# Expert tiles of 128 slots with three weight buffers, in place of 256 slots with two

## The chip, the cores and the metric

One core of a Trainium2 chip runs the whole kernel in one launch. Its engines are TensorE (PE; its weight loads are shown apart as PEld), VectorE (DVE), ScalarE (ACT), GpSimd (POOL) and SyncE (SP), and DMA queues that SyncE and GpSimd feed. The metric is the device time of one execution in microseconds (us), taken as the median of several runs. Everything is computed in float32.

## The reference

```python
scores = scale * q @ k.T ; masked by 32 x 32 blocks           # B=4, H=8, S=768, D=64
x = softmax(scores) @ v                                       # to (3072, 512)

xn = x / (norm(x) + 1e-6); en = expert_emb / (norm(expert_emb) + 1e-6)
logits = xn @ en.T / tau                                      # 8 experts
expert_idx = argmax(logits); gate_w = softmax(logits)[expert_idx]
for e in range(8):
    h = maximum(x[mask_e] @ w1[e], 0.0)                       # 512 -> 1024
    out[mask_e] = gate_w[mask_e] * (h @ w2[e])                # 1024 -> 512
```

Attention with a block mask gives 3072 rows of 512 values. Each row is sent to one of eight experts, a pair of matrices with a ReLU between them, and the result is multiplied by the row's gate.

## The kernel before

The program has three stages. **Attention** runs over 192 units (4 sequences, 8 heads, 6 chunks of 128 queries): `score` multiplies a chunk by the keys (L184), `turn_probs` transposes the exponentials on TensorE (L201), `attend` multiplies them by the values (L219). After each sequence `route` finds every row's expert, gate and rank and writes the rows with their gates to `x_dram`. **`dispatch`** then sorts: it gives every row a slot in expert order, each expert's rows being padded to a multiple of `G` slots. `NG` is the largest number of tiles that any routing can need, (3072 + 8 * (G - 1)) // G, and the loop over tiles always runs to `NG`: 19 tiles at G = 256. Tiles that hold no row are computed like the others.

**The expert stage** is the one that the change touches. `fetch(i)` issues what tile i needs: SyncE issues two DMAs of 2 MB, `w1` (L354) and `w2` (L356), from the expert whose number it has read into a register, and GpSimd issues one indirect DMA for each 128 slots (L361), which gathers rows from `x_dram`. `expert_tile(i)` then

- transposes the gathered rows on TensorE into `xg_ps` (L375) and copies them to `xgt`, one half by VectorE (L378) and one by ScalarE (L379);
- multiplies them by `w1` into `hp` (L386): 8 blocks `f` of 128 hidden values, each a sum over 4 pieces `d`, in two PSUM tiles of four blocks. `w1` is the stationary operand, and the slots are the moving columns, 256 of them. When four blocks are done, ScalarE takes the ReLU of two of them (L388) and VectorE of the other two (L389), into `h`;
- multiplies `h` by `w2` into `yp` (L394), 128 slots at a time: `h` is stationary, 512 columns of `w2` move, summed over the 8 blocks `f`;
- multiplies by the gate on VectorE into `y` (L397) and has GpSimd scatter `y` to the output by an indirect DMA (L399).

Every float32 matmul of the program but the transposes stands in the trace as two records, each with a weight load of its own, so the 32 matmuls of L386 are 64 records a tile and the 16 of L394 are 32; a transpose is one record. Weights lie in a pool of two buffers each for `w1` and `w2`, and `fetch(i + 1)` stands ahead of `expert_tile(i)` in the program. Each engine works through its own instructions in program order; semaphores, put in by the tile framework, order the engines among each other.

Of the kernel before, what the change touches and what calls it, by code (L numbers as in the profile page):

```python
# [10 lines left out]
F32 = mybir.dt.float32  # L11
I32 = mybir.dt.int32
ACT = mybir.ActivationFunctionType
ALU = mybir.AluOpType
# [3 lines left out]
P = 128  # L18
B, H, S, D = 4, 8, 768, 64
BLK = 32  # L20
NB = S // BLK  # attention blocks per sequence
NRAND = 3
NC = S // P  # chunks of 128 tokens; token p * NC + c of a sequence is row p of chunk c
NPAIR = H // 2
N = B * S
NT = B * NC
DM, E, F = H * D, 8, 1024
ND, NF = DM // P, F // P
G = 256  # slots of an expert tile: every expert's tokens are padded to a multiple of it
GS = G // P  # L30
NG = (N + E * (G - 1)) // G  # the most expert tiles that any routing can need
NS = NG * GS
XW = DM + 1  # a token's row: its activations and its gate
SCALE = 1.0 / float(D) ** 0.5
NEG = -1.0e9

# [40 lines left out]


def build_mask(k):
    """Rows that extend the contraction of q and k: the key's block one-hot against the  # L80
    query block's mask row (0 where it attends, NEG where not)."""
    nc, pool = k.nc, k.setup
    ids = pool.tile([NB, NRAND], I32, name="ids")
    words = dataclasses.replace(k.blocks.tensor, shape=[NB, 2 * NRAND], dtype=I32)
    with nc.allow_non_contiguous_dma(reason="low words of the block numbers"):
        nc.sync.dma_start(out=ids, in_=bass.AP(tensor=words, offset=0, ap=[[2 * NRAND, NB], [2, NRAND]]))
    ids_f = pool.tile([NB, NRAND], F32, name="ids_f")
    nc.vector.tensor_copy(out=ids_f, in_=ids)

    dif = iota(k, "dif", [NB, NB], [[1, NB]], mult=-1)  # L90
    col = iota(k, "col", [NB, NB], [[1, NB]])
    row = iota(k, "row", [NB, NB], [[0, NB]], mult=1)
    m = pool.tile([NB, NB], F32, name="m")
    nc.vector.tensor_tensor(out=m, in0=dif, in1=dif, op=ALU.mult)
    nc.vector.tensor_scalar(out=m, in0=m, scalar1=1.5, scalar2=None, op0=ALU.is_le)
    for val in (0.0, float(NB - 1)):
        for pos in (col, row):
            nc.vector.scalar_tensor_tensor(out=m, in0=pos, scalar=val, in1=m, op0=ALU.is_equal, op1=ALU.max)
    for r in range(NRAND):
        nc.vector.scalar_tensor_tensor(out=m, in0=col, scalar=ids_f[:, r:r + 1], in1=m,  # L100
                                       op0=ALU.is_equal, op1=ALU.max)
    nc.vector.tensor_scalar(out=m, in0=m, scalar1=1.0, scalar2=-NEG, op0=ALU.subtract, op1=ALU.mult)

    oh = pool.tile([P, NC, NB], F32, name="oh_blk")
    nc.gpsimd.memset(oh, 1.0)
    nc.gpsimd.affine_select(out=oh, in_=oh, pattern=[[1, NC], [-BLK, NB]], compare_op=ALU.is_ge,
                            fill=0.0, base=0, channel_multiplier=NC)
    nc.gpsimd.affine_select(out=oh, in_=oh, pattern=[[-1, NC], [BLK, NB]], compare_op=ALU.is_ge,
                            fill=0.0, base=BLK - 1, channel_multiplier=-NC)
    kr = k.big.tile([P, 1024], F32, name="kr", tag="big")  # L110
    for c in range(NC):
        nc.tensor.transpose(kr[0:NB, c * P:(c + 1) * P], oh[:, c, :], k.ident)
    krow = pool.tile([NB, S], F32, name="krow")
    nc.vector.tensor_copy(out=krow, in_=kr[0:NB, 0:S])
    qr = k.big.tile([P, 1024], F32, name="qr", tag="big")
    for lo, hi in ((0, 512), (512, S)):
        nc.tensor.matmul(qr[0:NB, lo:hi], lhsT=m, rhs=krow[:, lo:hi], start=True, stop=True)

    k.sides = []
    for i in range(2):  # L120
        side = {}
        for name, rows, copy in (("q", qr[0:NB, 0:S], nc.scalar.copy), ("k", krow, nc.vector.tensor_copy)):
            for h in range(2):
                side[name, h] = k.const.tile([D + NB, S], F32, name=f"{name}{h}_{i}")
                copy(out=side[name, h][D:D + NB, :], in_=rows)
        k.sides.append(side)
# [103 lines left out]


def route(k, b):
    """Expert, gate and rank within the expert for the tokens of one sequence."""
    nc, p, x = k.nc, k.rp, k.x[b]
    nrm = p.tile([P, NC], F32, name="nrm")
    for c in range(NC):
# [7 lines left out]
    for c2 in range(0, NC, 2):  # L244
        ps = k.big.tile([P, 2 * ND, P], F32, name="xt_ps", tag="big")
        for i in range(2 * ND):
            c, d = c2 + i // ND, i % ND
            nc.tensor.transpose(ps[:, i, :], x[:, c, d * P:(d + 1) * P], k.ident)
        xt = p.tile([P, 2 * ND, P], F32, name="xt")
        nc.vector.tensor_copy(out=xt, in_=ps)  # L250
        for c in (c2, c2 + 1):
            for d in range(ND):
                nc.tensor.matmul(lg[:, c, :], lhsT=xt[:, (c - c2) * ND + d, :], rhs=k.en[:, d, :],
                                 start=(d == 0), stop=(d == ND - 1))

    def wide(t):
# [15 lines left out]
    gate = p.tile([P, NC], F32, name="gate")  # L272
# [5 lines left out]
        out=k.x_dram[b * S:(b + 1) * S, :].rearrange("(p c) w -> p (c w)", c=NC),  # L278
        in_=x.rearrange("p c w -> p (c w)"),
    )  # L280

    for c in range(NC):
        t = b * NC + c
# [6 lines left out]


def dispatch(k):
    """Slots in expert order: the token of each slot (N where none is), the expert of each tile."""
    nc, p = k.nc, k.dp
    cp = k.small.tile([P, 512], F32, name="cp", tag="small")
    nc.tensor.matmul(cp[:, 0:E], lhsT=k.ones, rhs=k.seen[:, NT, :], start=True, stop=True)
# [6 lines left out]
    need = p.tile([P, E], F32, name="need")  # L303
# [46 lines left out]
def fetch(k, i):  # L350
    nc = k.nc
    e = nc.values_load(k.expert[0:1, i:i + 1], engines=(mybir.EngineType.SP,), min_val=0, max_val=E - 1)
    w1 = k.wp.tile([P, ND, F], F32, name="w1", tag="w1")
    nc.sync.dma_start(out=w1, in_=k.w1[bass.ds(e, 1), :, :].rearrange("o (c p) f -> p (o c) f", p=P))  # L354
    w2 = k.wp.tile([P, NF, DM], F32, name="w2", tag="w2")
    nc.sync.dma_start(out=w2, in_=k.w2[bass.ds(e, 1), :, :].rearrange("o (c p) m -> p (o c) m", p=P))  # L356
    xs = []
    for s in range(GS):
        x = k.gp.tile([P, XW], F32, name="xg", tag="xg")
        t = i * GS + s  # L360
        nc.gpsimd.indirect_dma_start(  # L361
            out=x[:, :], out_offset=None, in_=k.x_dram[:, :],
            in_offset=bass.IndirectOffsetOnAxis(ap=k.slot[:, t:t + 1], axis=0),
        )
        xs.append(x)
    k.fetched[i] = (w1, w2, xs)


def expert_tile(k, i):
    nc = k.nc  # L370
    w1, w2, xs = k.fetched.pop(i)
    ps = k.big.tile([P, ND, GS, P], F32, name="xg_ps", tag="big")
    for d in range(ND):
        for s in range(GS):
            nc.tensor.transpose(ps[:, d, s, :], xs[s][:, d * P:(d + 1) * P], k.ident)  # L375
    xt = k.mp.tile([P, ND, G], F32, name="xgt", tag="xgt")
    half = ND // 2
    nc.vector.tensor_copy(out=xt[:, 0:half], in_=ps[:, 0:half].rearrange("p d s t -> p d (s t)"))  # L378
    nc.scalar.copy(out=xt[:, half:ND], in_=ps[:, half:ND].rearrange("p d s t -> p d (s t)"))  # L379

    h = k.mp.tile([P, NF, G], F32, name="h", tag="h")
    for f0 in range(0, NF, 4):
        hp = k.big.tile([P, 4, G], F32, name="hp", tag="big")
        for f in range(4):
            for d in range(ND):
                nc.tensor.matmul(hp[:, f, :], lhsT=w1[:, d, (f0 + f) * P:(f0 + f + 1) * P], rhs=xt[:, d, :],  # L386
                                 start=(d == 0), stop=(d == ND - 1))
        nc.scalar.activation(h[:, f0:f0 + 2], hp[:, 0:2], ACT.Relu)  # L388
        nc.vector.tensor_scalar(out=h[:, f0 + 2:f0 + 4], in0=hp[:, 2:4], scalar1=0.0, scalar2=None, op0=ALU.max)  # L389

    for s in range(GS):
        yp = k.small.tile([P, DM], F32, name="yp", tag="small")
        for f in range(NF):
            nc.tensor.matmul(yp, lhsT=h[:, f, s * P:(s + 1) * P], rhs=w2[:, f, :],  # L394
                             start=(f == 0), stop=(f == NF - 1))
        y = k.gp.tile([P, DM], F32, name="y", tag="y")
        nc.vector.tensor_scalar(out=y, in0=yp, scalar1=xs[s][:, DM:XW], scalar2=None, op0=ALU.mult)  # L397
        t = i * GS + s
        nc.gpsimd.indirect_dma_start(  # L399
            out=k.out[:, :], out_offset=bass.IndirectOffsetOnAxis(ap=k.slot[:, t:t + 1], axis=0),  # L400
            in_=y[:, :], in_offset=None, bounds_check=N - 1, oob_is_err=False,
        )


@with_exitstack
def kernel(
# [14 lines left out]
    n = Net()  # L421
# [38 lines left out]

    with tc.tile_pool(name="dp", bufs=1) as n.dp:
        dispatch(n)
    n.wp = ctx.enter_context(tc.tile_pool(name="wp", bufs=2))
    n.gp = ctx.enter_context(tc.tile_pool(name="gp", bufs=4))
    n.mp = ctx.enter_context(tc.tile_pool(name="mp", bufs=2))
    fetch(n, 0)
    for i in range(NG):
        if i + 1 < NG:
            fetch(n, i + 1)
        expert_tile(n, i)  # L470


# [30 lines left out]
```

## Time and profile before

| what | us |
|---|---|
| median of 3 runs (lowest, highest) | 1352.59 (1351.52, 1358.27) |
| profiled execution, its span | 1351.6 |
| PE busy in the span | 1293.4 |
| PEld busy | 989.1 |
| DVE, ACT, POOL busy | 410.5, 358.3, 89.4 |

The profiled execution is shown by its span, from the first to the last instruction. The times of the runs are counted for a whole execution, and their median stands 1.0 us above the span. A row of the timeline gives start, duration, engine, line, operation, tiles and how many instructions were merged; in brackets stands how long the engine was idle before it, and which instruction ended that. The durations of matmul records overlap, so the pace of TensorE is read from the starts of the groups that follow each other, and not from the durations.

### The profile page before, as it was taken

Reading aid. Unit: us, or ns where it says so; the run is one execution under the profiler, and the core shown is the slowest. Engines: PE = TensorE matmul, PEld = TensorE weight load, DVE = VectorE, ACT = ScalarE, POOL = GpSimd, SP = SyncE. Lnnn points to the kernel's source line nnn. Section 1 sums busy time; section 2 is a strip of 40 time slices with the busy share of each in tenths; the row PEclk is TensorE's granted clock in tenths of the full one; section 3 lists DMA queues with packets and bytes.
Section 4 is the critical chain, followed back from the end, with each engine's and each line's share of the span. In section 5 each row is a group of like instructions: output and inputs, shape, how many; then the busy total and the mean of one; then the engine's idle time right before and its main releaser. Section 6 shows DMA issues by size and latency. Waiting matters only on the chain. (4 is left out here: it accounts for less than half of the span.)

```text
span 1351.6 us, 16579 instructions
## 1 busy us (share of the span) xinstructions
PE 1293.4 (96%) x6952; PEld 989.1 (73%) x6952; DVE 410.5 (30%) x619; ACT 358.3 (27%) x660; POOL 89.4 (7%) x125
## 2 busy tenths in 40 slices
PE   6999999999999999999999499999999999999997
PEld 4888888888888888888888466666666666666664
DVE  4444453444444444444444401111111111111110
ACT  3444443444434444444444000000000000000000
POOL 1000000000000000000000101111111111111110
PEclk9999998999979999899999589999999999999999
DMA  3010111111011010110000375544544554454420
GB/s 129 24 36 13 36 36 51 33 36 36 24 60 36 24 36 13 36 48 12 1 1 1 122 283 170 201 161 152 192 170 171 177 202 165 145 197 170 148 71 0
DMA packets 49696, 122.24 MB, mean 90 GB/s; under 512 B 3660, under 2 KB 15948, under 8 KB 49110
## 3 DMA queue, kind: packets, MB, share of 16 engines
q1 hardware_dynamic: 43542, 104.89, 22.1%
q0 software_dynamic: 6080, 16.28, 3.4%
q8 instruction: 55, 0.90, 0.3%
q14 instruction: 19, 0.16, 0.0%
HBM read 108.56 MB, written 16.27 MB: 92 GB/s over the span
## 5 line engine op out<-in xcount | busy, mean ns | idle before, releaser
L184 PE MATMUL sc<-k,q 88*128 88x512 f32 (+1 forms) x768 | 294.6, 506 | 0.0
L386 PE MATMUL hp<-xgt,w 128*128 128x256 f32 x1216 | 270.4, 383 | 14.9 <-DVE xgt L378 14.9
L219 PE MATMUL av<-vld,et 128*128 128x64 f32 x2304 | 278.8, 271 | 0.3 <-ACT et L206 0.3
L189 DVE TENSOR_REDUCE nm<-sc 128x1 f32<-128x768 f32 x192 | 183.9, 958 | 296.9 <-PE sc L184 296.6
L219 PEld LDWEIGHTS av<-vld,et 128*128 128x128 f32 x2304 | 272.3, 192 | 0.5 <-ACT et L206 0.5
L386 PEld LDWEIGHTS hp<-xgt,w 128*128 128x128 f32 x1216 | 231.5, 192 | 50.8 <-DVE xgt L378 19.6
L394 PE MATMUL yp<-w,h 128*128 128x512 f32 x608 | 264.0, 592 | 0.0
L191 ACT ACTIVATE e<-sc,nm 128x768 f32<-128x768 f32 x192 | 173.5, 904 | 172.0 <-DVE nm L189 172.0
L394 PEld LDWEIGHTS yp<-w,h 128*128 128x128 f32 x608 | 115.5, 190 | 137.3 <-issue 136.3
L184 PEld LDWEIGHTS sc<-k,q 88*128 88x128 f32 x768 | 133.1, 194 | 92.2 <-issue 92.1
L201 PE MATMUL et_ps<-ident,e 128*128 128x128 f32 x1152 | 161.6, 277 | 0.8 <-ACT e L191 0.8
L206 ACT COPY et<-et_ps 128x768 f32<-128x768 f32 x128 | 101.8, 796 | 208.2 <-PE et_ps L201 208.2
L201 PEld LDWEIGHTS et_ps<-ident,e 128*128 128x128 f32 x1152 | 141.3, 144 | 18.9 <-ACT e L191 1.2
L389 DVE TENSOR_SCALAR h<-hp 128x512 f32<-128x512 f32 x38 | 26.3, 692 | 271.0 <-ACT h L388 271.0
L397 DVE TENSOR_SCALAR y<-yp,xg 128x512 f32<-128x512 f32 x38 | 28.5, 750 | 221.6 <-PE yp L394 221.6
L379 ACT COPY xgt<-xg_ps 128x512 f32<-128x512 f32 x19 | 11.1, 585 | 300.1 <-DVE xgt L378 300.1
L388 ACT ACTIVATE h<-hp 128x512 f32<-128x512 f32 x38 | 22.7, 597 | 248.0 <-PE hp L386 248.0
L399 POOL DMA_INDIRECT out_dram<-y,slot x38 | 38.4, 1011 | 487.5 <-DVE y L397 487.5
L204 DVE COPY et<-et_ps 128x768 f32<-128x768 f32 x64 | 60.7, 948 | 0.7 <-PE et_ps L201 0.7
L239 POOL TENSOR_TENSOR nrm<-nrm,half 128x6 f32<-128x6 f32 x4 | 5.3, 1330 | 684.1 <-ACT sq L238 684.1
L361 POOL DMA_INDIRECT xg<-x_dram,slot x38 | 37.2, 978 | 31.8 <-DVE slot L347 20.5
L191 ACT ACTIVATION_READ_ACCUMULATOR e<-sc,nm 128x1 f32 x192 | 38.1, 199 | 0.0
(114 smaller groups left out, 437.1 us busy)
## 6 DMA issues: line engine op xcount, KB each, us to landing
w<-in_moe_w_dram SPq DMA_DIRECT2D x38, 2048.0 KB, 9.0
x_dram<-x SPq DMA_DIRECT2D x4, 1539.0 KB, 5.8
kld<-in_k_dram SPq DMA_DIRECT2D x16, 384.0 KB, 3.2
qld<-in_q_dram SPq DMA_DIRECT2D x16, 384.0 KB, 3.6
vld<-in_v_dram SPq DMA_DIRECT2D x16, 384.0 KB, 3.2
xg<-x_dram,slot POOLq DMA_INDIRECT x38, 6.7
out_dram<-y,slot POOLq DMA_INDIRECT x38, 2.8
x_dram<-zero SPq DMA_DIRECT2D x1, 2.0 KB
```

The costliest lines, as they stand in the source:

```text
L184: nc.tensor.matmul(ps[:, lo:hi], lhsT=side["q", hh][:, c * P:(c + 1) * P], rhs=side["k", hh][:, lo:hi], start=True, stop=True)
L189: nc.vector.tensor_reduce(out=nm, in_=ps[:, 0:S], axis=AX.X, op=ALU.max, negate=True)
L191: nc.scalar.activation(e, ps[:, 0:S], ACT.Exp, bias=nm[:, 0:1], scale=1.0, accum_out=k.sums[u // NC][:, c:c + 1])
L201: nc.tensor.transpose(ps[:, c * P:(c + 1) * P], e[:, c * P:(c + 1) * P], k.ident)
L204: nc.vector.tensor_copy(out=et, in_=ps[:, 0:S])
L206: nc.scalar.copy(out=et, in_=ps[:, 0:S])
L219: nc.tensor.matmul(k.av[:, c, :], lhsT=et[:, kc * P:(kc + 1) * P], rhs=v[:, hh, kc, :], start=(kc == 0), stop=(kc == NC - 1))
L361: nc.gpsimd.indirect_dma_start(out=x[:, :], out_offset=None, in_=k.x_dram[:, :], in_offset=bass.IndirectOffsetOnAxis(ap=k.slot[:, t:t + 1] ...
L386: nc.tensor.matmul(hp[:, f, :], lhsT=w1[:, d, (f0 + f) * P:(f0 + f + 1) * P], rhs=xt[:, d, :], start=(d == 0), stop=(d == ND - 1))
L394: nc.tensor.matmul(yp, lhsT=h[:, f, s * P:(s + 1) * P], rhs=w2[:, f, :], start=(f == 0), stop=(f == NF - 1))
L397: nc.vector.tensor_scalar(out=y, in0=yp, scalar1=xs[s][:, DM:XW], scalar2=None, op0=ALU.mult)
L399: nc.gpsimd.indirect_dma_start(out=k.out[:, :], out_offset=bass.IndirectOffsetOnAxis(ap=k.slot[:, t:t + 1], axis=0), in_=y[:, :], in_offse ...
```

## The change

`G` becomes 128, and so a tile has one group of 128 slots, `NG` becomes 31, and the weight pool has three buffers. Two tiles are fetched ahead of the loop, and `fetch(i + 2)` stands ahead of `expert_tile(i)`. Within a tile, `xg_ps` moves to the PSUM pool of `yp` and is copied by VectorE alone. One PSUM tile `hp` of two banks holds all eight blocks `f`; ScalarE takes the ReLU of blocks 0 to 3 and VectorE of blocks 4 to 7.

```diff
-G = 256
+G = 128
...
 def expert_tile(k, i):
...
-    ps = k.big.tile([P, ND, GS, P], F32, name="xg_ps", tag="big")
+    ps = k.small.tile([P, ND, P], F32, name="xg_ps", tag="small")
...
+        nc.tensor.transpose(ps[:, d, :], x[:, d * P:(d + 1) * P], k.ident)
+    xt = k.mp.tile([P, ND, P], F32, name="xgt", tag="xgt")
+    nc.vector.tensor_copy(out=xt, in_=ps)
...
+    hp = k.big.tile([P, NF, P], F32, name="hp", tag="big")
+    h = k.mp.tile([P, NF, P], F32, name="h", tag="h")
+    half = NF // 2
+    for f in range(NF):
+        for d in range(ND):
+            nc.tensor.matmul(hp[:, f, :], lhsT=w1[:, d, f * P:(f + 1) * P], rhs=xt[:, d, :],
+                             start=(d == 0), stop=(d == ND - 1))
+        if f == half - 1:
+            nc.scalar.activation(h[:, 0:half], hp[:, 0:half], ACT.Relu)
+    nc.vector.tensor_scalar(out=h[:, half:NF], in0=hp[:, half:NF], scalar1=0.0, scalar2=None, op0=ALU.max)
...
+    for f in range(NF):
+        nc.tensor.matmul(yp, lhsT=h[:, f, :], rhs=w2[:, f, :], start=(f == 0), stop=(f == NF - 1))
...
-    n.wp = ctx.enter_context(tc.tile_pool(name="wp", bufs=2))
+    n.wp = ctx.enter_context(tc.tile_pool(name="wp", bufs=3))
...
     fetch(n, 0)
+    fetch(n, 1)
     for i in range(NG):
-        if i + 1 < NG:
-            fetch(n, i + 1)
+        if i + 2 < NG:
+            fetch(n, i + 2)
         expert_tile(n, i)
```

TensorE, one tile near the end of the program before; a number behind `w` names one buffer's contents, and brackets name the semaphores that an instruction waits for (of the gather `DMASW`, of the weights `DMAHW`, and of the engines).

```order
L375 MATMUL xg_ps<-ident,xg 128x128 [waits DMASW5_49,PE_49]
L375 MATMUL xg_ps<-ident,xg 128x128 [waits DMASW7_49]
L375 MATMUL xg_ps<-ident,xg 128x128 x6
L386 MATMUL hp<-xgt,w_7205 128x256 [waits DMAHW0_49,DVE_49]
L386 MATMUL hp<-xgt,w_7205 128x256
L386 MATMUL hp<-xgt,w_7205 128x256 [waits Activation_49]
L386 MATMUL hp<-xgt,w_7205 128x256 x13
L386 MATMUL hp<-xgt,w_7205 128x256 [waits PE_49]
L386 MATMUL hp<-xgt,w_7205 128x256 x15
L394 MATMUL yp<-w_7207,h 128x512 [waits DMAHW1_49,Activation_49]
```

The same place after the change.

```order
L375 MATMUL xg_ps<-ident,xg 128x128 [waits DMASW7_49,PE_49]
L375 MATMUL xg_ps<-ident,xg 128x128 x3
L384 MATMUL hp<-xgt,w_7735 128x128 [waits DMAHW2_49,DVE_49]
L384 MATMUL hp<-xgt,w_7735 128x128 x15
L384 MATMUL hp<-xgt,w_7735 128x128 [waits Activation_49]
L384 MATMUL hp<-xgt,w_7735 128x128 x15
L392 MATMUL yp<-w_7737,h 128x512 [waits DMAHW3_49]
L392 MATMUL yp<-w_7737,h 128x512 x3
L392 MATMUL yp<-w_7737,h 128x512 [waits DVE_49]
L392 MATMUL yp<-w_7737,h 128x512 x3
```

The wait for ScalarE has moved from the third matmul by `w1` (the one that reads ScalarE's half of `xgt`) to the seventeenth, the first of block 4. In the built program the count that it waits for is the one that the ReLU of this same tile's blocks 0 to 3 raises.

SyncE, the first weight DMAs before.

```order
L354 DMA w_5732<-in_moe_w_dram 128x4x1024
L356 ISA
L356 DMA w_5734<-in_moe_w_dram 128x8x512
L354 ISA
L354 DMA w_5750<-in_moe_w_dram 128x4x1024
L356 ISA
L356 DMA w_5752<-in_moe_w_dram 128x8x512
L354 ISA
L354 DMA w_5847<-in_moe_w_dram 128x4x1024
```

And after the change.

```order
L354 DMA w_5732<-in_moe_w_dram 128x4x1024
L356 ISA
L356 DMA w_5734<-in_moe_w_dram 128x8x512
L354 ISA
L354 DMA w_5748<-in_moe_w_dram 128x4x1024
L356 ISA
L356 DMA w_5750<-in_moe_w_dram 128x8x512
L354 ISA
L354 DMA w_5764<-in_moe_w_dram 128x4x1024
L356 ISA
L356 DMA w_5766<-in_moe_w_dram 128x8x512
```

Three pairs of loads now stand ahead of the first one that has to wait for a buffer, where there were two; behind them the pairs go on one for one as before, 31 in all instead of 19.

## Rows read from the trace of the kernel before

**Rows 1.** Page, span in 40 slices: granted TensorE clock and DMA, tenths.

```profile
PEclk9999998999979999899999589999999999999999
DMA  3010111111011010110000375544544554454420
```

**Rows 2.** Stages: us, each engine's busy time (instructions), clock, DMA share, GB/s.

```profile
769.16:781.31 12.15, 2.20 (x8) 1.53 (x9) 0.78 (x2) 0.00 (x0) 4.03 (x4) 0.50 0.89 326
781.31:798.12 16.81, 16.81 (x64) 14.33 (x65) 0.69 (x1) 1.18 (x2) 0.00 (x0) 0.82 0.86 328
798.12:1328.60 530.48, 516.38 (x1874) 343.70 (x1873) 64.35 (x90) 32.02 (x54) 69.58 (x70) 1.00 0.46 164
...
1342.33:1351.63 9.30, 0.16 (x1) 0.00 (x0) 0.75 (x1) 0.00 (x0) 0.98 (x1) 0.75 0.00 0
```

**Rows 3.** Timeline of one whole expert tile, the second: start, duration, instruction.

```profile
798.12 13.90 PE L394 MATMUL yp<-w,h 128*128 128x512 f32 x32
...
811.85 1.04 PE L375 MATMUL xg_ps<-ident,xg 128*128 128x128 f32 x8
...
812.06 0.75 DVE L397 TENSOR_SCALAR y<-yp,xg 128x512 f32<-128x512 f32 x1 [6.12 <-PE yp L394]
812.93 0.69 DVE L378 COPY xgt<-xg_ps 128x512 f32<-128x512 f32 x1
...
813.68 14.08 PE L386 MATMUL hp<-xgt,w 128*128 128x256 f32 x64 [0.79 <-DVE xgt L378]
...
820.89 0.60 ACT L388 ACTIVATE h<-hp 128x512 f32<-128x512 f32 x1 [6.65 <-PE hp L386]
821.52 0.69 DVE L389 TENSOR_SCALAR h<-hp 128x512 f32<-128x512 f32 x1 [7.90 <-ACT h L388]
...
827.59 7.89 PE L394 MATMUL yp<-w,h 128*128 128x512 f32 x18
...
827.79 0.60 ACT L388 ACTIVATE h<-hp 128x512 f32<-128x512 f32 x1 [6.31 <-PE hp L386]
```

**Rows 4.** Attention by line and shape: count, busy us, mean ns, idle before.

```profile
L219 PE MATMUL av<-vld,et 128*128 128x64 f32 x2304 | 278.8, 271 | 0.3 <-ACT et L206 0.3
L219 PEld LDWEIGHTS av<-vld,et 128*128 128x128 f32 x2304 | 272.3, 192 | 0.5 <-ACT et L206 0.5
...
L201 PE MATMUL et_ps<-ident,e 128*128 128x128 f32 x1152 | 161.6, 277 | 0.8 <-ACT e L191 0.8
L201 PEld LDWEIGHTS et_ps<-ident,e 128*128 128x128 f32 x1152 | 141.3, 144 | 18.9 <-ACT e L191 1.2 <-issue 0.6
```

**Rows 5.** Timeline of one attention unit on PE.

```profile
402.13 1.45 PE L219 MATMUL av<-vld,et 128*128 128x64 f32 x12
403.42 1.51 PE L184 MATMUL sc<-k,q 88*128 88x512 f32 x4
404.76 0.82 PE L201 MATMUL et_ps<-ident,e 128*128 128x128 f32 x6
405.42 1.45 PE L219 MATMUL av<-vld,et 128*128 128x64 f32 x12
```

**Rows 6.** Expert stage, 800 to 1300 us, by line: L386's weight loads.

```profile
L386 PEld LDWEIGHTS hp<-xgt,w 128*128 128x128 f32 x1088 | 205.3, 190 | 44.6 <-DVE xgt L378 17.4
```

**Rows 7.** The DMAs of `w1` (L354), from issue to landing, over the run.

```profile
DMA to landing us min/median/max: 7.4/7.9/21.3
```

**Rows 8.** The same for `w2`.

```profile
DMA to landing us min/median/max: 8.9/9.7/21.8
```

**Rows 9.** A stage (columns as in rows 2) while only weights and gathers load.

```profile
772.00:794.00 22.00, 14.89 (x53) 12.25 (x54) 1.38 (x2) 1.18 (x2) 2.49 (x3) 0.65 1.03 391
```

**Rows 10.** Timeline of PE where the first expert tile begins.

```profile
777.66 0.45 PE L375 MATMUL xg_ps<-ident,xg 128*128 128x128 f32 x1 [8.64 <-issue]
778.77 1.75 PE L375 MATMUL xg_ps<-ident,xg 128*128 128x128 f32 x7 [0.67 <-DMA xg<-x_dram,slot]
```

**Rows 11.** Page, DMA issues: the gathers, with the median us to landing.

```profile
xg<-x_dram,slot POOLq DMA_INDIRECT x38, 6.7
```

More of the change, by code (lines that the diff above doesn't have):

```diff
@@ L371, in expert_tile @@
     w1, w2, xs = k.fetched.pop(i)
-    ps = k.big.tile([P, ND, GS, P], F32, name="xg_ps", tag="big")
+    x = xs[0]
+    ps = k.small.tile([P, ND, P], F32, name="xg_ps", tag="small")
     for d in range(ND):
[L374 to L402, printed above, removed]
+        nc.tensor.transpose(ps[:, d, :], x[:, d * P:(d + 1) * P], k.ident)
@@ new lines, in expert_tile @@
+    nc.vector.tensor_scalar(out=h[:, half:NF], in0=hp[:, half:NF], scalar1=0.0, scalar2=None, op0=ALU.max)
+    yp = k.small.tile([P, DM], F32, name="yp", tag="small")
+    for f in range(NF):
+        nc.tensor.matmul(yp, lhsT=h[:, f, :], rhs=w2[:, f, :], start=(f == 0), stop=(f == NF - 1))
+    y = k.gp.tile([P, DM], F32, name="y", tag="y")
+    nc.vector.tensor_scalar(out=y, in0=yp, scalar1=x[:, DM:XW], scalar2=None, op0=ALU.mult)
+    nc.gpsimd.indirect_dma_start(
+        out=k.out[:, :], out_offset=bass.IndirectOffsetOnAxis(ap=k.slot[:, i:i + 1], axis=0),
+        in_=y[:, :], in_offset=None, bounds_check=N - 1, oob_is_err=False,
+    )
```

## The prediction

> **What bounds the kernel now.** Read the slices of the page first [rows 1]: the expert stage is the right-hand part, where DMA stands at 4 to 5 tenths and TensorE's clock at full. The table by stages puts numbers on it [rows 2]. From 798.12 to 1328.60 us TensorE is busy in 516 of 530 us at clock 1.00, while VectorE, ScalarE and GpSimd have 64, 32 and 70 us and the DMA engines 0.46 of the time. TensorE bounds the stage. The stretch is 18 tiles, 530.48 / 18 = 29.47 us each.
>
> The timeline of one tile [rows 3] shows where they go. The matmuls by `w2` take from 798.12 to 811.85, 13.73 us for 32 records, 0.429 each. From there to the first matmul by `w1` at 813.68 it is 1.83 us: eight transposes, while VectorE first drains `y` (0.75) and then copies its half of `xgt` (0.69). The matmuls by `w1` take from 813.68 to 827.59, 13.91 us for 64 records. ScalarE drains the last four blocks 0.20 after 827.59; set back by the same 0.20, its start at 820.89 puts the end of the first four blocks at 820.69. So the first 32 records took 7.01 us and the second 32 took 6.90: 0.2156 each and 0.11 for starting up.
>
> **The change, part by part.** *Slots.* Tiles of 128 make 31 groups of 128 slots where there were 19 * 2 = 38. Everything whose cost goes with slots falls by 7 in 38, and everything paid once a tile is paid 31 times instead of 19.
>
> *The matmuls by `w2`* go with slots: 8 matmuls, 16 records, 16 * 0.429 = 6.86 us a tile.
>
> *The matmuls by `w1`* decide the case. They keep their 64 records a tile and their 64 weight loads, and each record moves 128 columns, not 256. By columns a record costs half of 0.2156, 0.108 us. The load does not shrink, and the trace of before has no float32 matmul of 128 columns, so it is bounded by its neighbours. In attention, the records of L219 move only 64 columns, a quarter of 0.2156 or 0.054, yet 12 of them take from 402.13 to 403.42, 0.1075 each [rows 5]: there the weight load sets the pace, and streaming hides behind it entirely. The transposes of L201 move 128 columns and load 128; six take from 404.76 to 405.42, 0.110 each, with a load record of 144 ns against 192 [rows 4, 5]: there streaming sets the pace and a shorter load hides. In L386 a load of 190 ns hides inside 0.2156 [rows 6]. The new record is the case between: load and stream are about 0.108 each. If they go on side by side, the pace is 0.1075 to 0.110; I take 0.109, because both neighbours hide the smaller part without a remainder. The other end is that they follow each other: 0.108 + 0.108 = 0.216, no gain from half the columns.
>
> A rule of the Trainium skill speaks for that end: "TensorE: Matmul & The Clock Gate", Part 3, The mechanism, has weight loads overlap with matmuls in flight only where the row groups differ, and all these use all 128 rows. By it the sum would be 31 * 64 * 0.107 = 212 us higher, 1521 us. The trace contradicts it: L219 would then need 0.1075 + 0.054 = 0.16 a record and needs 0.1075 [rows 5].
>
> *A new wait.* One `hp` now holds all eight blocks, and ScalarE's ReLU of blocks 0 to 3 stands in the program before the matmuls of block 4. In TensorE's order the first matmul of block 4 waits for ScalarE, and the count is that of this tile's own ReLU, though the two touch different banks. Before, two `hp` tiles kept them apart: the second four blocks ran while ScalarE and VectorE drained the first [rows 3]. The trace of before has the same kind of wait elsewhere: VectorE's ReLU starts at 821.52, just as ScalarE's of the same tile ends (820.89 + 0.60), though their halves differ [rows 3]. Price, from rows 3: 0.20 from the end of the matmuls to ScalarE's start, 0.60 for the same 128x512, and 0.06 until TensorE goes on (as from the end of `xgt` at 813.62 to 813.68): 0.86 us a tile in which all that stands behind on TensorE waits, 31 * 0.86 = 27 us. As the restart costs 0.11 twice now, each half of `hp` is 0.10 + 32 * 0.109 = 3.59 us. Between nothing hidden and some, 0.80 to 1.0 is my bound.
>
> *The step between tiles.* Four transposes take the place of eight, about 0.5 us less, but VectorE drains `y` before `xgt` as before, and its copy is 128x512 as before. `xgt` can start at most the 0.12 earlier that lies between the two [rows 3]. I take 1.80 us, with 1.70 to 1.85 as bounds. ScalarE's copy goes; it was off the path. VectorE's ReLU of blocks 4 to 7 ends about 0.9 us after the matmuls and is first needed after four blocks by `w2`, 3.4 us later: hidden.
>
> *Loads.* A tile still needs 2 * 2 MB of weights, now every 16.7 us instead of every 29.47. Before, 0.46 * 29.47 = 13.6 us a tile is what all DMA engines needed, with two gathers and two scatters [rows 2]; it is less now, so they have room. In the first burst they move 391 GB/s [rows 9], 10.7 us for 4.19 MB. A load lands 8 to 10 us after its issue, 22 in the burst [rows 7, 8], and with three buffers it is issued two tiles ahead of its use, over 33 us. On SyncE only loads queue behind a load that waits. On GpSimd the gather of tile i + 2 stands behind the scatter of tile i - 1, so it is issued just after tile i begins, more than a tile ahead of its use, and takes 6.7 [rows 11]. The six loads ahead of the loop delay nothing that is needed soon: the third of four landed about 791.7 before (issued at 770.34, 21.3 later), and tile 1 needs it at 799. The third buffer itself I cost at nothing in either direction; with two, a load would still be issued some 25 us ahead.
>
> *The sum.* A tile: 1.80 + 3.59 + 0.86 + 3.59 + 6.86 = 16.70 us. That is more per 128 slots than before (29.47 / 2 = 14.74), and pays because there are 31 and not 38: 31 * 16.70 = 518 against 19 * 29.47 = 560. The ends: the first transposes wait only for the first gather, and four instead of eight run at half clock, so that the first matmul by `w1` moves from 781.31 to about 779.5 [rows 2, 10]. The first tile runs part of the way at half clock, which cost 16.81 - 13.91 = 2.9 us; I keep that. So: 779.5 + 3.59 + 0.86 + 3.59 + 2.9 = 790.4; thirty tiles more, 501.0, to 1291.4; the last 6.86, to 1298.3; the end as before, 9.30 [rows 2], gives a span of 1307.6. By the same terms before is 798.12 + 530.48 + 13.73 + 9.30 = 1351.6, its span, and the median of the runs is 1.0 above that. **1309 us**, 3.2% less.
>
> **The rivals.** *Load and stream hinder each other when they are equally long (slower).* Every record of before has one clearly longer part to hide the other in; the new one has none. Each hundredth of a us on the record costs 31 * 64 * 0.01 = 19.8 us. The gain is gone at 0.131, a fifth above my 0.109. If half a load stays uncovered, the record is 0.162, the tile 3.4 us longer, and the time 1309 + 105 = 1414. Against it speak L219 and L201, whose paces hold no remainder above 2 ns [rows 5]. The Trainium skill has figures for this in the same page, Part 2, Back-to-back issue gap: at 128 columns a stream of load and matmul pairs paces 81 ns, against about 56 for matmuls alone; as an estimate, that ratio would make the record 0.156 and the time 1402. No run here shows that shape yet. I give 11%.
>
> *The DMAs become the bound.* If the two loads of a tile followed each other with their single landing times, 7.9 + 9.7 = 17.6 us a tile, the time would be 1309 + 30 * 0.9 = 1336. Against it: 391 GB/s when several are queued [rows 9]. 4%.
>
> *The new wait is longer than its parts,* because TensorE's queue of loads has to start again: if it costs double, 1336. 8%. That the wait isn't there at all, for 1282, I give 2%, since it stands in the program.
>
> *The clock falls.* Two pauses of some 0.9 us in 16.7 instead of one in 29.47; at half clock on the `w1` matmuls the tile would be 7 us longer, over 1500. The clock stayed at 1.00 through all pauses of 0.79 [rows 2, 3]. 2%.
>
> **How the numbers follow.** The forecast has 73%. Its own bounds: 0.1075 a record without start-up, 1.70 between tiles and 0.80 for the wait make 16.24 a tile and 1295; 0.125 a record makes 1341. The range 1295 to 1341 takes in the DMA rival and the longer wait and leaves out the equal-length rival, the clock and the missing wait. A measurement tells about 0.5% from no change: faster below 1345.8, slower above 1359.4. The first, the DMAs, the longer and the missing wait are faster, 87%; of the equal-length rival and the clock I count 3% as no change and 10% as slower.
>
> **What would show it.** In the timeline of a tile after: the 32 records of each half of `hp` in about 3.6 us; between them TensorE idle 0.6 to 0.9 us, released by ScalarE; a tile every 16.7 us; clock 1.00; DMA share 0.7 to 0.8 and no wait of TensorE for a weight DMA. If the halves take 4.3 us or more, the forecast is wrong by its pace; if the tiles are 17.6 apart with waits for DMA, by its loads.

## The result, and the profile after

The changed kernel takes **1308.74 us** (median of 4 runs, 1302.42 to 1318.14), the kernel before, run again beside it, 1355.12 (median of 4); the ratio is 0.9665, with a 95% interval of 0.9613 to 0.9717. The forecast was 1309. The profiled execution has a span of 1305.1 us.

The slices of the page of the changed kernel, in the form of [rows 1]: the clock is back at full in the expert stage, and DMA stands at 7 to 9 tenths where it stood at 4 to 5.

```profile
PEclk9999998999989999989999859999999999999999
DMA  4000101100011011010000049988877888778830
```

The stages after, against [rows 2] (us, busy time and instructions of PE, PEld, DVE, ACT and POOL, clock, DMA share, GB/s). They run from the first load to the first matmul by `w1`, to the first by `w2`, then thirty tiles, the last matmuls by `w2`, and the end.

```profile
769.28:778.92 9.64, 1.11 (x4) 0.74 (x5) 0.72 (x2) 0.00 (x0) 4.03 (x4) 0.50 0.89 316
778.92:789.85 10.93, 10.24 (x64) 10.05 (x65) 0.00 (x0) 0.60 (x1) 0.00 (x0) 0.74 1.03 392
789.85:1290.10 500.25, 449.50 (x2523) 320.39 (x2522) 61.22 (x90) 17.92 (x30) 56.73 (x57) 1.00 0.77 275
1290.10:1296.96 6.86, 6.86 (x18) 2.84 (x16) 0.69 (x1) 0.00 (x0) 0.00 (x0) 1.00 0.00 0
1296.96:1305.10 8.14, 0.16 (x1) 0.00 (x0) 0.75 (x1) 0.00 (x0) 0.99 (x1) 0.69 0.00 0
```

Thirty tiles in 500.25 us are 16.67 each. TensorE is now busy for 449.50 of them, 90%, where it was 516.38 of 530.48, 97% [rows 2]: it loses more in pauses than before and yet ends sooner, because it does 31 groups of 128 slots and not 38.

One tile of the timeline, against [rows 3] (start, duration, instruction, and in brackets the idle time before it and what ended that). L375 are the transposes, L384 the matmuls by `w1`, L392 those by `w2`, L387 and L388 the two ReLUs.

```profile
813.39 0.60 PE L375 MATMUL xg_ps<-ident,xg 128*128 128x128 f32 x4
...
813.60 0.75 DVE L394 TENSOR_SCALAR y<-yp,xg 128x512 f32<-128x512 f32 x1 [6.11 <-PE yp L392]
814.26 0.68 DVE L377 COPY xgt<-xg_ps 128x512 f32<-128x512 f32 x1
...
815.00 3.84 PE L384 MATMUL hp<-xgt,w 128*128 128x128 f32 x32 [1.00 <-DVE xgt L377]
...
818.87 0.60 ACT L387 ACTIVATE h<-hp 128x512 f32<-128x512 f32 x1 [16.08 <-PE hp L384]
...
819.52 3.84 PE L384 MATMUL hp<-xgt,w 128*128 128x128 f32 x32 [0.69 <-ACT h L387]
...
823.20 7.03 PE L392 MATMUL yp<-w,h 128*128 128x512 f32 x16
...
830.07 0.60 PE L375 MATMUL xg_ps<-ident,xg 128*128 128x128 f32 x4
```

Three things are to be seen. The two halves of `hp` stand apart, and the second begins only when ScalarE's ReLU of the first has ended (818.87 + 0.60, then 819.52): the new wait. The second half takes from 819.52 to 823.20, 3.68 us for 32 records with 0.11 of starting up in it, where 32 records of 256 columns took 6.90 without [rows 3]: halving the columns nearly halved the time. And from 813.39 to 815.00 it is 1.61 us between tiles, where it was 1.83.

By the table of waits (engine, what waited for what, us in total, times, longest), the two pauses are all that TensorE waits for in the stage behind its first gather (7.9 us, once), in each tile once. No wait for a weight DMA is among its entries.

```profile
PE hp L384 <- DVE xgt L377: 31.0, 31, 1.0
...
PE hp L384 <- ACT h L387: 21.3, 31, 0.7
```

### The profile page after: what moved, and what is told of

It is laid out like the page before. It is cut to its first block, busy times and chain, and to the rows that moved or that the text cites. A ratio compares the mean times of both kernels' runs of the same rounds, so it can differ in the third digit from the quotient of the medians.

```text
span 1305.1 us, 17883 instructions
## 1 busy us (share of the span) xinstructions
PE 1211.5 (93%) x7580; PEld 957.1 (73%) x7580; DVE 405.7 (31%) x617; ACT 343.3 (26%) x634; POOL 75.6 (6%) x111
## 5 line engine op out<-in xcount | busy, mean ns | idle before, releaser
L384 PE MATMUL hp<-xgt,w 128*128 128x128 f32 x1984 | 240.7, 280 | 52.3 <-DVE xgt L377 31.0
L219 PE MATMUL av<-vld,et 128*128 128x64 f32 x2304 | 278.8, 271 | 0.3 <-ACT et L206 0.3
L384 PEld LDWEIGHTS hp<-xgt,w 128*128 128x128 f32 x1984 | 228.9, 194 | 65.7 <-DVE xgt L377 37.3
L219 PEld LDWEIGHTS av<-vld,et 128*128 128x128 f32 x2304 | 272.4, 192 | 0.5 <-ACT et L206 0.5
L392 PE MATMUL yp<-w,h 128*128 128x512 f32 x496 | 218.0, 592 | 0.0
L392 PEld LDWEIGHTS yp<-w,h 128*128 128x128 f32 x496 | 91.9, 190 | 103.8 <-issue 103.8
L387 ACT ACTIVATE h<-hp 128x512 f32<-128x512 f32 x31 | 18.5, 597 | 520.0 <-PE hp L384 520.0
L388 DVE TENSOR_SCALAR h<-hp 128x512 f32<-128x512 f32 x31 | 21.4, 692 | 267.1 <-PE hp L384 267.1
L394 DVE TENSOR_SCALAR y<-yp,xg 128x512 f32<-128x512 f32 x31 | 23.3, 751 | 189.3 <-PE yp L392 189.3
L395 POOL DMA_INDIRECT out_dram<-y,slot x31 | 31.3, 1011 | 458.7 <-DVE y L394 458.7
L174 DVE COPY k<-turn 64x768 f32<-64x768 f32 x32 | 30.2, 945 | 23.8 <-PE turn L169 23.8
L375 PEld LDWEIGHTS xg_ps<-ident,xg 128*128 128x128 f32 x124 | 15.7, 143 | 23.8 <-issue 15.8
```

Source lines behind the costliest of these rows:

```text
L174: nc.vector.tensor_copy(out=dst[0:D, :], in_=ps[0:D, 0:S])
L219: nc.tensor.matmul(k.av[:, c, :], lhsT=et[:, kc * P:(kc + 1) * P], rhs=v[:, hh, kc, :], start=(kc == 0), stop=(kc == NC - 1))
L384: nc.tensor.matmul(hp[:, f, :], lhsT=w1[:, d, f * P:(f + 1) * P], rhs=xt[:, d, :], start=(d == 0), stop=(d == ND - 1))
L392: nc.tensor.matmul(yp, lhsT=h[:, f, :], rhs=w2[:, f, :], start=(f == 0), stop=(f == NF - 1))
L394: nc.vector.tensor_scalar(out=y, in0=yp, scalar1=x[:, DM:XW], scalar2=None, op0=ALU.mult)
L395: nc.gpsimd.indirect_dma_start(out=k.out[:, :], out_offset=bass.IndirectOffsetOnAxis(ap=k.slot[:, i:i + 1], axis=0), in_=y[:, :], in_offse ...
```

## The experiments

**The new wait taken away.** One edit of the changed kernel: two PSUM tiles of four blocks each.

```diff
-    hp = k.big.tile([P, NF, P], F32, name="hp", tag="big")
...
+    for f0 in (0, half):
+        hp = k.big.tile([P, half, P], F32, name="hp", tag="big")
```

> The changed kernel with one edit: `hp` is two PSUM tiles of four blocks each instead of one of eight, so that the matmuls of block 4 no longer wait for ScalarE's ReLU of blocks 0 to 3. Theory (the wait is paid in full, since nothing stands beside it on TensorE): the pause of 0.69 us released by ScalarE, 0.85 from slot to slot, vanishes from every tile, with the second start-up of about 0.1; the tile falls from 16.67 to about 15.75 us, the time by 31 * 0.9 = 28 us to about 1280. Rival (the pause only moves: the first matmul by w2 then waits for ScalarE, or TensorE waits for a PSUM buffer): a pause of the same length shows elsewhere in the tile and the time stays within 7 us of 1309.

Measured: 1279.59 us, ratio 0.9445 (0.9413 to 0.9478). The timeline of TensorE shows all 64 records in one piece, 7.25 us from 812.12 to 819.37, and nothing in place of the pause; from there to the next tile's matmuls by `w1` everything is as in the changed kernel.

```profile
812.12 7.41 PE L385 MATMUL hp<-xgt,w 128*128 128x128 f32 x64 [1.00 <-DVE xgt L377]
819.37 7.03 PE L394 MATMUL yp<-w,h 128*128 128x512 f32 x16
826.24 0.60 PE L375 MATMUL xg_ps<-ident,xg 128*128 128x128 f32 x4
827.84 4.40 PE L385 MATMUL hp<-xgt,w 128*128 128x128 f32 x37 [1.01 <-DVE xgt L377]
```

A tile is 827.84 - 812.12 = 15.72 us, 0.95 less. The wait came from the tile framework's order for one shared tile, not from the data, and was paid in full: 29 us of the time.

**The third buffer taken away.** The changed kernel with the weight pool and the order of fetches of before.

```diff
-    n.wp = ctx.enter_context(tc.tile_pool(name="wp", bufs=3))
+    n.wp = ctx.enter_context(tc.tile_pool(name="wp", bufs=2))
```

> The changed kernel with the weight pool back at two buffers and one tile fetched ahead; tiles of 128 slots stay. Theory (the third buffer is worth nothing, since a load is still issued some 25 us ahead of its use and lands in about 10): the tile stays 16.67 us apart, no wait of TensorE for a weight DMA, time within 7 us of 1309. Rival (with two buffers the loads bunch up and the tile waits for them): tiles of 17.6 us or more, 1336 or above, with waits for DMA ahead of L384 or L392.

Measured: 1305.29 us, ratio 0.9641 (0.9606 to 0.9677). In TensorE's timeline the tile begins at 810.71 and at 827.38, 16.67 us apart, with the two pauses of the changed kernel and no other.

```profile
810.71 3.84 PE L384 MATMUL hp<-xgt,w 128*128 128x128 f32 x32 [1.00 <-DVE xgt L377]
815.23 3.84 PE L384 MATMUL hp<-xgt,w 128*128 128x128 f32 x32 [0.69 <-ACT h L387]
...
827.38 3.84 PE L384 MATMUL hp<-xgt,w 128*128 128x128 f32 x32 [1.00 <-DVE xgt L377]
```

**The third buffer alone**, in the kernel before, with tiles of 256 slots.

```diff
-    n.wp = ctx.enter_context(tc.tile_pool(name="wp", bufs=2))
+    n.wp = ctx.enter_context(tc.tile_pool(name="wp", bufs=3))
...
+    fetch(n, 1)
...
-            fetch(n, i + 1)
+            fetch(n, i + 2)
```

> The kernel before with one edit: three weight buffers and two tiles fetched ahead; tiles of 256 slots stay. Theory (loads were hidden before and are hidden now): 29.47 us a tile as before, time within 0.5% of the kernel before. Rival (the longer burst at the start delays the first tile, or the earlier loads collide with gathers): up to 10 us slower, seen ahead of the first tile.

Measured: 1357.25 us, ratio 1.0005 (0.9982 to 1.0028). Its tiles by `w2` begin at 802.02 and 831.50, 29.48 us apart. So the whole difference belongs to the tiles of 128 slots and what was rewritten inside them, in both directions of the test.

**Pace against columns.** The question on which the forecast hung: does a weight load of 128 columns hide behind a stream of as many? The changed kernel, with a number of moving columns that changes from tile to tile.

```diff
+    cols = (64, 96, 112, 128, 144, 192)[i % 6]
...
-            nc.tensor.matmul(hp[:, f, :], lhsT=w1[:, d, f * P:(f + 1) * P], rhs=xt[:, d, :],
+            nc.tensor.matmul(hpf[:, o:o + cols], lhsT=w1[:, d, f * P:(f + 1) * P], rhs=xtf[:, r:r + cols],
```

> Measures the pace of the records by w1 against the number of moving columns: tile i moves 64, 96, 112, 128, 144 or 192 columns in turn (i modulo 6) with 128 stationary columns always, so the products by w1 are not the reference's; below 128 columns one matmul of 512 columns fills each half of the PSUM tile first. Theory (load and stream go on side by side, the longer sets the pace): 64, 96 and 112 columns pace as L219 did, about 0.1075 us; 128 at 0.11; 144 at 0.121 and 192 at 0.162, that is 0.108 per 128 columns. Rival (they hinder each other when about equal): a hump around 112 to 144 columns above both lines, by 0.01 us or more; fully one after the other would give 0.16 at 64 and 0.27 at 192.

TensorE's timeline (L390 the matmuls by `w1`, L398 those by `w2`, L386 the filling ones). The pace is read from the start of a second half of 32 records to the start of L398 behind it; where TensorE waited just ahead of the half (128 columns and more), the 0.11 of starting up is taken off.

```profile
818.53 3.71 PE L390 MATMUL hp<-xgt,w 128*128 128x96 f32 x32
822.08 7.06 PE L398 MATMUL yp<-w,h 128*128 128x512 f32 x16
...
836.91 3.72 PE L390 MATMUL hp<-xgt,w 128*128 128x112 f32 x32
840.47 7.04 PE L398 MATMUL yp<-w,h 128*128 128x512 f32 x16
...
853.48 3.84 PE L390 MATMUL hp<-xgt,w 128*128 128x128 f32 x32 [0.69 <-ACT h L393]
857.16 7.03 PE L398 MATMUL yp<-w,h 128*128 128x512 f32 x16
...
870.50 4.19 PE L390 MATMUL hp<-xgt,w 128*128 128x144 f32 x32 [0.69 <-ACT h L393]
874.53 7.03 PE L398 MATMUL yp<-w,h 128*128 128x512 f32 x16
...
889.15 5.47 PE L390 MATMUL hp<-xgt,w 128*128 128x192 f32 x32 [0.69 <-ACT h L393]
894.46 7.03 PE L398 MATMUL yp<-w,h 128*128 128x512 f32 x16
...
1024.91 3.68 PE L390 MATMUL hp<-xgt,w 128*128 128x64 f32 x32
1028.42 7.09 PE L398 MATMUL yp<-w,h 128*128 128x512 f32 x16
```

| moving columns | us for 32 records | us a record | by columns alone (0.2156 at 256) |
|---|---|---|---|
| 64 | 3.51 | 0.110 | 0.054 |
| 96 | 3.55 | 0.111 | 0.081 |
| 112 | 3.56 | 0.111 | 0.094 |
| 128 | 3.68 - 0.11 | 0.112 | 0.108 |
| 144 | 4.03 - 0.11 | 0.123 | 0.121 |
| 192 | 5.31 - 0.11 | 0.163 | 0.162 |

(The time of this kernel, 1372.62 us, says nothing, since its tiles differ in work.) Up to 128 columns the pace hardly changes, 0.110 to 0.112; above, it goes with the columns. The small rise up to 128 is that of a group's first records, which follow each other at another step. Counted from the third record on, 30 records take 3.35 us at 64, at 96 and at 112 columns alike (1025.07 to 1028.42, 818.73 to 822.08, 837.12 to 840.47), 0.112 each, and at 128 columns the 31 from the second on take 3.47 (853.69 to 857.16), 0.112 too. The same timeline at 64 columns, narrowed so that the group begins with its third record:

```profile
1025.07 3.51 PE L390 MATMUL hp<-xgt,w 128*128 128x64 f32 x30
```

So there is no hump at 128, where load and stream are nearly equal, and nothing like the 0.162 of a load half uncovered. That the weight load sets the 0.112 is argued, as it is the part of a record that stays the same when the columns shrink; no run changes the load itself.

The prediction set two figures of the Trainium skill against the trace. By the rule of "TensorE: Matmul & The Clock Gate", Part 3, The mechanism, that loads overlap matmuls in flight only where the row groups differ, these records would take 0.22 us; the same section also has loads into a background weight buffer pulled ahead, and the prediction left that out. By the ratio taken from Part 2, Back-to-back issue gap, they would take 0.156, as an estimate. This run has 0.112 for full-height float32 records, and the measurement decides.

**Half the loads.** The changed kernel, every odd tile with the weights of the even tile ahead of it.

```diff
+    if i % 2 == 0:
         w1 = k.wp.tile([P, ND, F], F32, name="w1", tag="w1")
...
+        k.shared = w1, w2
+    w1, w2 = k.shared
```

> The changed kernel with every odd tile using the weights of the even tile ahead of it, so that 32 of the 62 weight DMAs are left and the products of odd tiles are not the reference's where the expert differs. Theory (loads are hidden and cost TensorE nothing): tiles 16.67 us apart as with all loads, and the time within 0.7% of 1309; the DMA share about halves. Rival (loads slow the matmuls through shared memory ports, or delay gathers and scatters): shorter tiles; 0.1 us less a tile would show in the timeline.

Measured: 1310.31 us in one run, span 1308.6. The same stretch, 820 to 1220 us, first in the changed kernel and then in this one (columns as in the stages above):

```profile
820.00:1220.00 400.00, 359.40 (x2017) 256.10 (x2016) 48.97 (x72) 14.34 (x24) 47.73 (x48) 1.00 0.82 289
```

```profile
820.00:1220.00 400.00, 359.39 (x2016) 256.09 (x2016) 48.96 (x72) 14.33 (x24) 47.51 (x49) 1.00 0.45 156
```

The DMA share falls from 0.82 to 0.45, and TensorE's busy time and count of instructions are the same to 0.01 us and one instruction. Its tiles are 16.67 us apart as before (first matmuls by `w1` at 818.50 and 835.17). The loads cost the matmuls nothing.

**The copy on ScalarE.** The changed kernel with the copy of `xgt` off VectorE.

```diff
-    nc.vector.tensor_copy(out=xt, in_=ps)
+    nc.scalar.copy(out=xt, in_=ps)
```

> The changed kernel with the copy of `xgt` on ScalarE instead of VectorE. Theory (between tiles TensorE waits for VectorE's drain of `y` and then its copy, one behind the other): the copy no longer stands behind the drain; from the end of the matmuls by w2 to the first by w1 it takes 0.44 for the transposes, 0.20 to ScalarE's start, 0.59 and 0.06, that is 1.3 instead of 1.60 us, and the time falls by 31 * 0.3 = 9 us. Rival (the step is set by the transposes and the copy alone): 1.60 us as before.

Measured: 1302.74 us in one run. In the timeline the copy now runs beside VectorE's drain of `y` and not behind it:

```profile
817.13 0.60 PE L375 MATMUL xg_ps<-ident,xg 128*128 128x128 f32 x4
...
817.33 0.75 DVE L394 TENSOR_SCALAR y<-yp,xg 128x512 f32<-128x512 f32 x1 [6.11 <-PE yp L392]
817.82 0.58 ACT L377 COPY xgt<-xg_ps 128x512 f32<-128x512 f32 x1 [11.29 <-PE xg_ps L375]
...
818.46 3.84 PE L384 MATMUL hp<-xgt,w 128*128 128x128 f32 x32 [0.73 <-ACT xgt L377]
```

The step is 818.46 - 817.13 = 1.33 us instead of 1.61. The timeline settles it; a single time could not, since 31 * 0.28 = 9 us is less than the spread of the changed kernel's own runs.

**Both pauses filled.** Two PSUM tiles for `hp`, and the transposes of tile i + 1 with their copy between tile i's matmuls by `w1` and by `w2`; then the same with two weight buffers.

```diff
+def turn_tile(k, i):                  # the transposes and the copy to xgt
...
+    xt = k.turned.pop(i)
...
+    if i + 1 < NG:
+        turn_tile(k, i + 1)
     yp = k.small.tile([P, DM], F32, name="yp", tag="small")
```

> The changed kernel with two edits: `hp` in two PSUM tiles (as in the run with that edit alone), and the four transposes of tile i + 1 with their copy to `xgt` placed between tile i's matmuls by w1 and by w2, so that VectorE's drain of `y` and copy of `xgt` lie beside the matmuls. Theory (TensorE bounds, and the two pauses are all that it loses beside its records): a tile is 64 * 0.1115 + 0.11 + 4 * 0.11 + 6.87 = 14.55 us, 2.1 less than 16.67; the time falls by 31 * 2.1 = 66 us to about 1243. The loads then need 4.72 MB per 14.55 us, 324 GB/s. Rival (the DMAs become the bound as the tiles get shorter): tiles of 15 us or more with TensorE waiting for DMA, 1257 or above.

> The same with two weight buffers and one tile fetched ahead. Theory (a load is issued 14.55 + 6.87 = 21.4 us ahead of its use and lands in 10 to 11): same time as with three buffers within 0.5%, about 1243. Rival (with loads every 14.55 us the third buffer starts to matter): waits for DMA ahead of the matmuls, 2 us or more a tile, 1305 or above.

Measured: **1238.22 us**, ratio 0.9146 (0.9118 to 0.9174), with three buffers, and 1241.56, ratio 0.9178 (0.9125 to 0.9231), with two. TensorE's timeline with three:

```profile
807.87 7.03 PE L402 MATMUL yp<-w,h 128*128 128x512 f32 x16
814.74 7.31 PE L391 MATMUL hp<-xgt,w 128*128 128x128 f32 x64
821.88 0.60 PE L374 MATMUL xg_ps<-ident,xg 128*128 128x128 f32 x4
822.32 7.03 PE L402 MATMUL yp<-w,h 128*128 128x512 f32 x16
```

No pause is left: 822.32 - 807.87 = 14.45 us a tile, made of 7.14 + 0.44 + 6.87. The DMAs now move 319 GB/s at a share of 0.87, and still TensorE waits for no weight load; with two buffers the tile is the same (815.98 to 830.43, 14.45), so that even here the third buffer buys nothing that can be measured.

**The same edit with 256 slots,** in the kernel before: transposes and copies ahead of the matmuls by `w2`.

> The kernel before, tiles of 256 slots, with the transposes of tile i + 1 and their copies placed between tile i's matmuls by w1 and by w2. It tells what the number of padded slots is worth once no pause is left in either tile. Theory (the gain of tiles of 128 is 31 groups of 128 slots computed in place of 38, against weight loads that no longer hide): a tile is 64 * 0.2156 + 0.11 + 8 * 0.11 + 13.73 = 28.5 us, 0.95 less than before, so 19 * 0.95 = 18 us off the kernel before, about 1337, and 1.075 times the time with tiles of 128 and the same edit. Rival (the gain came mostly from pauses that fell away with smaller tiles): below 1290.

Measured: 1336.94 us, ratio 0.9868 (0.9790 to 0.9946). Its tiles:

```profile
808.50 13.98 PE L392 MATMUL hp<-xgt,w 128*128 128x256 f32 x64
822.31 1.04 PE L375 MATMUL xg_ps<-ident,xg 128*128 128x128 f32 x8
823.18 13.90 PE L402 MATMUL yp<-w,h 128*128 128x512 f32 x32
836.92 13.98 PE L392 MATMUL hp<-xgt,w 128*128 128x256 f32 x64
```

A tile is 836.92 - 808.50 = 28.42 us, 14.21 for 128 slots, against 14.45 with tiles of 128. Once no pause is left in either, 128 slots cost almost the same in both (64 records at 0.112 in place of half of 0.2156 make the 0.2 us of difference). The times are 1336.94 / 1238.22 = 1.080 apart (1.079 by their ratios to the kernel before), and the 38 groups against 31 make 38 * 14.21 - 31 * 14.45 = 92 of these 99 us; the rest is within the spread of their runs.

## Why the prediction was right

*The sum by its terms,* in us a tile. Forecast and measured come from the same places, the measured ones from the tile shown above.

| term | forecast | measured |
|---|---|---|
| from the end of `w2` to the first matmul by `w1` | 1.80 | 1.61 |
| first half of `hp` | 3.59 | 3.67 |
| the new wait | 0.86 | 0.85 |
| second half of `hp` | 3.59 | 3.68 |
| matmuls by `w2` | 6.86 | 6.87 |
| tile | 16.70 | 16.68 |

(The end of the first half is set 0.20 ahead of ScalarE's start at 818.87, as in the prediction.)

*The pace of the records* came out at 0.1115 to 0.112, not at 0.109, and outside the 0.1075 to 0.110 that the prediction gave for load and stream side by side: 5 us in all. The argument from the neighbours, one with the shorter stream and one with the shorter load, was right in kind: each hides the other. What was mis-sized is the pace of L219. Its 12 records were read as one mean, 0.1075 [rows 5], but the first two take 0.17 us together, and the ten behind them (403.42 - 402.30) / 10 = 0.112 each. The timeline of [rows 5], narrowed so that the group begins with its third record:

```profile
402.30 1.28 PE L219 MATMUL av<-vld,et 128*128 128x64 f32 x10
403.42 0.65 PE L184 MATMUL sc<-k,q 88*128 88x512 f32 x1
```

So the trace of before already held the 0.112 that the new records take.

*The new wait* was read from the order of the instructions and priced from three rows: 0.86 forecast, 0.85 in the timeline. The run without it fell by 29 us, where the expectation was 28.

*The step between tiles* is the other term outside its own bounds (1.70 to 1.85). I had VectorE's copy start behind the drain of `y` with a gap of up to 0.12, and took the 0.12 of [rows 3] as the most that could go. That gap had belonged to the eight transposes: they ended at 811.85 + 1.04 = 812.89, and the copy began at 812.93. With four, the copy starts at 814.26, while `y` still drains until 814.35; the next instruction of VectorE begins before the last has ended. This took back 6 us, and with the 5 of the pace the two misses nearly cancel. The total is closer than its parts, by luck. It is luck too that the median lies 0.3 us from the forecast: the runs spread over 16 us, and the profiled one has a span of 1305.1 where the sum gave 1307.6, and a time 1.8 above its span where the sum added 1.0.

*The loads.* The forecast put the DMA share at 0.7 to 0.8 and expected no wait; it is 0.77 in the thirty tiles, 0.82 in their middle, with no wait. The run with half the loads and the three on the third buffer bear out that they cost nothing and that the buffer is worth nothing.

*The ends.* The first matmul by `w1` came at 778.92 (forecast 779.5), the first by `w2` at 789.85 (790.4). The end took 8.14, not 9.30; this was not looked into.

*The rivals.* That load and stream hinder each other is excluded by the pace at six widths; that the DMAs become the bound, by half the loads and by 319 GB/s without a wait for a weight load; that the new wait costs more than its parts, by the run without it; and the clock stood at 1.00 through two pauses a tile.

## What to carry to other kernels

Where tiles are padded to a fixed size and TensorE bounds them, count what is computed in padding: here 38 groups of slots became 31. Smaller tiles paid because a record of 128 columns takes about half of what one of 256 takes, 0.112 us against 0.2156, though its weight load is as large. Below 128 the matmuls by `w1` would gain nothing, since the pace stays at 0.11. Each pause inside a tile is paid once a tile, so smaller tiles make it dearer: two pauses of 0.85 and 1.2 us cost 70 us of 1309 (the changed kernel less the one with both filled), and a second PSUM tile and another order took both away. Two engines that work on different halves of one on-chip tile can be made to wait for each other by whoever orders them; look for the wait in the order of the instructions before it is in the trace.

## What was not expected of the hardware

**The clock fell while TensorE was busy.** In the run with changing widths, TensorE went from a tile of 192 columns into one of 64 at clock 1.00, and the second half of that tile ran at 0.50, the lower of the two levels (1.2 against 2.4 GHz). Its pauses, 1.0 and 0.7 us, were those of every tile. The rows are the two halves of that tile, and then the two halves of the next tile of 64 columns (columns as in the stages above):

```profile
902.93:907.00 4.07, 4.07 (x31) 3.59 (x31) 0.00 (x0) 0.00 (x0) 1.61 (x2) 1.00 0.90 295
908.26:916.84 8.58, 8.58 (x34) 7.55 (x35) 0.00 (x0) 0.00 (x0) 0.00 (x0) 0.50 0.28 110
1018.61:1022.70 4.09, 4.09 (x31) 3.61 (x31) 0.00 (x0) 0.00 (x0) 1.62 (x2) 1.00 0.90 299
1023.94:1028.42 4.48, 4.48 (x34) 4.00 (x35) 0.00 (x0) 0.00 (x0) 0.00 (x0) 1.00 0.46 178
```

Its 32 records took 6.72 us (910.12 to 916.84) where the same 32 of the next such tile took 3.51. Busy time did not tell the stretches apart: TensorE is shown as fully busy in all four. The next tile of 64 columns and the two after it, with the same instructions and the same pauses, stayed at 1.00 throughout. In routing it fell too with TensorE busy; in the changed kernel, first 20 us of attention ahead of routing and then a stretch of it:

```profile
170.00:190.00 20.00, 20.00 (x146) 17.07 (x144) 9.89 (x13) 9.13 (x16) 0.00 (x0) 1.00 0.12 40
...
200.00:212.00 12.00, 12.00 (x52) 9.98 (x53) 3.65 (x12) 3.19 (x7) 0.47 (x3) 0.57 0.00 1
```

The run with two weight buffers has the same code up to there and stood at 1.00 in the same stretch. What brings the clock down in one case and not in the other, these runs don't settle.

**The runs of one kernel differ by the clock.** The four runs of the changed kernel have spans from 1300.4 to 1316.4 us, and their mean granted clocks, 0.974 and 0.963, go with them. As an estimate, at 0.974 the core is at half clock for 2 * 0.026 * 1300.4 = 68 us, at 0.963 for 2 * 0.037 * 1316.4 = 97; half of the 30 us between is lost work, 15 of the 16.0 us that the spans differ by. In the profiled run the thirty tiles stand at 1.00, and the dips lie in routing, in the sorting ahead of the tiles and at the end: in the first routing, from 190 to 230 us, it has 0.87. The run with two weight buffers, whose mean is 0.974, has 1.00 there. So this spread belongs to neither change, and a difference of one per cent between single runs says nothing without their clocks.
